# A tuned transformer block on one core: tile 1 in two pieces, x2 and x3 loaded behind weight block 2, tiles 4 to 7 normalized in pairs, the Gelu table preloaded, four DMA transposes ahead of the stores

## Chip, cores, metric

One core of one Trainium2 chip. The metric is the device time of one execution in us. A ratio is the mean time of one kernel's runs over that of the other's of the same rounds, so it is not quite the ratio of the medians quoted. The profile covers a somewhat shorter span than the device time (227.4 against 229.1 us for one run of the kernel before).

## The reference

```python
xn = layernorm(x)                       # x: 2048 x 512, bf16
s  = window_attention(xn, wqkv) @ wo    # 32 heads of 16, 8 keys at distances 0, 2, .. 14
g  = silu((gelu(xn @ w_gate) * (xn @ w_up)) @ w_down)   # 512 -> 1792 -> 512
return x + s * g
```

## The kernel before

The 2048 rows are worked on in four row blocks of four tiles of 128 rows. Each row block is normalized, transposed (xnT), projected to q, k, v, and goes through the gated layer and the attention. Row block 0's first projection is done half a row block at a time, so that it can begin when tiles 0 and 1 are there. x0 to x3 are the tiles as loaded. "Weight block k" (w0 to w3) is wqkv's rows 128k to 128k+127; one pass over it is 12 matmuls of 256 columns ("block k" below). It is multiplied with chunk k of each tile, that is the tile's columns 128k to 128k+127 after the transpose.

```python
    for i in range(2):                       # loads: x0 x1 w0 w1 x2 x3 w2 w3
        for t in (2 * i, 2 * i + 1):
            load_x(t)
        for k in (2 * i, 2 * i + 1):
            nc.sync.dma_start(out=wqkv_sb[:, k, :], in_=A_wqkv[k * P : (k + 1) * P, :])
    # ... cut: the other loads, constants ...
    first_stats(0); first_moments(0); first_stats(1); first_rstd(0); first_moments(1)
    normalize(0)
    transpose(0)                             # TensorE into PSUM, ScalarE copies to xnT
    first_rstd(1)
    normalize(1)
    warm_up(4, P)                            # matmuls on constants
    transpose(1, parts=2, copy=nc.vector.tensor_copy)
    for t in (2, 3):
        first_stats(t); first_moments(t)     # sqrt on ScalarE
    for t in (2, 3):
        first_rstd(t); normalize(t)
    for dk in range(NC):                     # blocks 0..3 for tiles 0 and 1
        for n, (fo, ps) in enumerate(pairs): # 2 pairs of v, 4 of q and k
            # ... cut: two matmuls on xnT[0][:, dk, 0:256] ...
            if dk == 2 and n in (2, 5):
                transpose(2 + (n == 5), copy=nc.vector.tensor_copy)
    for fo, ps in pairs:
        copy_out(0, fo, ps, 0, HQ, 2, nc.vector.tensor_copy if fo >= 8 else None)
    for t in range(TPQ, 2 * TPQ):
        moments(t)                           # then normalize(4..7) in the next loop
    # ... cut: second half (tiles 2 and 3), 48 matmuls into qkv_ps ...
    # block 1 and on: per-stage side work
    at(("glu", 1, 0), transpose_by_dma, 2 * TPQ + i)   # i = 0..3, SyncE's queue
    at(("glu", 2, 0), transpose_by_dma, 3 * TPQ + i)
```

The softmax here doesn't subtract the row's maximum and nothing guards it: scores larger than these inputs give would overflow.

## Time and profile before

| | kernel before | changed kernel |
|---|---|---|
| median, lowest to highest (us) | 229.41, 228.83 to 229.80 (6 runs) | 228.49, 228.35 to 229.03 (6 runs) |
| span of the profile | 227.4 | 226.7 |
| first useful matmul starts | 6.55 | 6.27 |
| second half of the projection starts | 12.45 | 11.98 |
| second u group of the gated layer starts | 20.93 | 20.25 |

(A u group is the four matmuls with w_up for 128 of the 1792 columns; a g group those with w_gate.) Three lines from the timeline of TensorE, kernel before (start, length, engine, line, operation, operands, count, in brackets the idle time and what ended it):

```profile
6.55 0.60 PE L554 MATMUL v_ps<-xnT,wqkv_sb 128*128 128x256 bf16 x4 [0.48 <-DVE xnT L225]
9.37 0.61 PE L554 MATMUL v_ps<-xnT,wqkv_sb 128*128 128x256 bf16 x4
12.45 0.27 PE L249 MATMUL qkv_ps<-xnT,wqkv_sb 128*128 128x256 bf16 x1
```

They are the starts of block 0, of block 2 and of the second half. A block without a wait takes 1.31 us, four transposes 0.22 us.

### The profile page before, as it was taken

What the parts mean: (1) busy time and instruction counts of PE and PEld (TensorE: products, weight loads), DVE (VectorE), ACT (ScalarE), POOL (GpSimd) and SP (SyncE); (2) the same over time, 40 slices, a digit from 0 to 9 for tenths busy, and PEclk for the clock granted to TensorE, in tenths of its full rate; (3) what the DMA queues carried; (4) which work ended last, traced back from release to release, by engine and by line L of the source; (5) the groups of instructions that cost most, each with busy time, mean ns of one, the idle gap of its engine ahead of it and who ended that gap; (6) DMA issues with size and microseconds to landing.
All of it is one profiled execution on the core that took longest, in us unless ns stands there. A gap on an engine that the chain in (4) does not pass through costs nothing.

```text
span 227.4 us, 3595 instructions
## 1 busy us (share of the span) xinstructions
PE 222.3 (98%) x1326; PEld 107.1 (47%) x1326; DVE 151.8 (67%) x278; ACT 132.2 (58%) x209; POOL 25.0 (11%) x67
## 2 busy tenths in 40 slices
PE   8999999999999999999999999999999999999993
PEld 4785444444444444444444444444444444444453
DVE  4696981899995588969904759924934348971434
ACT  4279769777531676766751466767763356756210
POOL 1027901000040000333700000000000000000000
PEclk9999999999999999999999999999999999999998
DMA  6999499941039911100219921100217950000011
GB/s 206 349 395 384 127 201 142 321 109 67 28 83 202 223 25 25 29 10 0 92 33 206 214 71 29 26 18 0 81 26 151 197 140 0 0 0 22 12 37 56
DMA packets 30130, 24.64 MB, mean 108 GB/s; under 512 B 10784, under 2 KB 29600, under 8 KB 30112
## 3 DMA queue, kind: packets, MB, share of 16 engines
q1 hardware_dynamic: 30112, 24.41, 44.3%
q8 instruction: 10, 0.16, 0.3%
q14 instruction: 8, 0.07, 0.1%
HBM read 18.74 MB, written 4.34 MB: 102 GB/s over the span
## 4 chain that ended last, share of the span: by engine, by line
PE 95%; DVE 1%; ACT 1%; DMA 1%; issue 0%; DVEq 0%
PE y_ps L443 21%; PE u_ps L249 21%; PE g_ps L249 21%; PE qkv_ps L249 16%; PE s_ps L459 6%; PE L_ps L338 3%; PE o_ps L406 3%; PE qk_ps L554 2%; DMA x_sb<-in_A_x_dram 1%; PE v_ps L554 1%; ACT L431 1%; DVE stats L182 1%; PE tr L214 1%; PE den_ps L358 0%; ACT ge L431 0%; ACT vst L273 0%
## 5 line engine op out<-in xcount | busy, mean ns | idle before, releaser
L249 PE MATMUL u_ps<-xnT,wu_sb 128*128 128x512 bf16 x224 | 57.5, 379 | 0.0
L249 PE MATMUL g_ps<-xnT,wg_sb 128*128 128x512 bf16 x224 | 57.5, 379 | 0.0
L443 PE MATMUL y_ps<-wd_sb,h 128*128 128x512 bf16 (+1 forms) x238 | 49.9, 367 | 0.0
L435 DVE TENSOR_TENSOR h<-ge,u 128x512 bf16<-128x512 bf16 x56 | 23.8, 425 | 30.7 <-ACT u L433 29.0
L433 ACT ACTIVATE u<-u_ps 128x512 bf16<-128x512 f32 x56 | 33.5, 598 | 16.4 <-PE u_ps L249 16.4
L431 ACT ACTIVATE ge<-g_ps 128x512 bf16<-128x512 f32 x56 | 33.5, 598 | 16.2 <-PE g_ps L249 16.0
L320 DVE TENSOR_TENSOR pk<-q_sb,k_sb 128x1024 bf16<-128x1024 bf16 (+1 forms) x56 | 38.9, 762 | 4.6 <-ACT k_sb L273 4.6
L392 DVE TENSOR_TENSOR pv<-E,v_arr 128x1024 bf16<-128x1024 bf16 (+1 forms) x48 | 39.8, 863 | 0.2 <-issue 0.2
L249 PE MATMUL qkv_ps<-xnT,wqkv_sb 128*128 128x512 bf16 (+1 forms) x192 | 37.0, 352 | 0.0
L443 PEld LDWEIGHTS <-h 128*128 128x128 bf16 x238 | 23.0, 98 | 25.9 <-issue 1.3
L249 PEld LDWEIGHTS <-wu_sb 128*128 128x128 bf16 x224 | 21.9, 98 | 26.6 <-issue 0.3
L249 PEld LDWEIGHTS <-wg_sb 128*128 128x128 bf16 x224 | 21.7, 98 | 26.3 <-issue 0.8
L451 ACT ACTIVATE sl<-y_ps 128x512 bf16<-128x512 f32 (+1 forms) x17 | 9.7, 572 | 32.6 <-PE y_ps L443 32.6
L249 PEld LDWEIGHTS <-wqkv_sb 128*128 128x128 bf16 x192 | 18.8, 98 | 17.5
L467 DVE TENSOR_TENSOR m<-s_ps,sl 128x512 bf16<-128x512 f32 (+1 forms) x17 | 11.1, 655 | 17.0 <-PE s_ps L459 17.0
L418 DVE TENSOR_TENSOR oT<-o_ps,rb 128x1024 bf16<-128x1024 f32 x8 | 9.4, 1220 | 13.8 <-DMA rb<-rs_d 13.8
L199 POOL TENSOR_TENSOR rstd<-rstd,mhalf 128x1 f32<-128x1 f32 x12 | 8.0, 663 | 69.9 <-DVE rstd L196 69.9
L459 PE MATMUL s_ps<-wo_sb,oT 128*128 128x512 bf16 (+1 forms) x68 | 14.8, 366 | 0.0
L273 ACT ACTIVATE vst<-qkv_ps 128x512 bf16<-128x512 f32 x14 | 8.4, 597 | 3.7 <-PE qkv_ps L249 3.7
L273 ACT ACTIVATE k_sb<-qkv_ps 128x512 bf16<-128x512 f32 x14 | 8.4, 601 | 3.2 <-PE qkv_ps L249 3.2
L273 ACT ACTIVATE q_sb<-qkv_ps 128x512 bf16<-128x512 f32 x14 | 8.3, 603 | 3.0 <-PE qkv_ps L249 3.0
L459 PEld LDWEIGHTS <-oT 128*128 128x128 bf16 x68 | 6.7, 98 | 7.2
(57 smaller groups left out, 131.4 us busy)
## 6 DMA issues: line engine op xcount, KB each, us to landing
v_arr<-vT SPq DMA_DIRECT2D x16, 520.0 KB, 8.5
vT<-vst SPq DMA_DIRECT2D x8, 256.0 KB, 2.2
out_dram<-o_t SPq DMA_DIRECT2D x15, 128.0 KB, 3.4
wg_sb<-in_B_w_gate_dram SPq DMA_DIRECT2D x2, 896.0 KB, 10.1
wu_sb<-in_B_w_up_dram SPq DMA_DIRECT2D x2, 896.0 KB, 11.0
wd_sb<-in_B_w_down_dram SPq DMA_DIRECT2D x1, 1792.0 KB, 11.5
wqkv_sb<-in_A_wqkv_dram SPq DMA_DIRECT2D x4, 384.0 KB, 4.9
x_sb<-in_A_x_dram SPq DMA_DIRECT2D x3, 512.0 KB, 10.5
```

Source lines behind the costliest of these rows:

```text
L249: nc.tensor.matmul(ps, lhsT=w[:, dk, lo : lo + P], rhs=xnT[j][:, dk, i0 : i0 + n], start=(dk == 0), stop=(dk == NC - 1),)
L273: nc.scalar.activation(out=dst, in_=ps, func=AF.Copy)
L320: nc.vector.tensor_tensor(out=st[j]["pk"][w][:, c0 : c0 + n, :], in0=st[j]["q"][:, c0 : c0 + n, :], in1=k_sb[j][:, c0 : c0 + n, off : off ...
L392: nc.vector.tensor_tensor(out=pv[:, d : d + n, :], in0=st[j]["E"][:, wh, :].unsqueeze(1).to_broadcast([P, n, TQ]), in1=st[j]["va"][:, 4 * ...
L418: nc.vector.tensor_tensor(out=oT[:, g : g + 2, :], in0=st[j]["o"][:, g : g + 2, :], in1=st[j]["rb"][:].unsqueeze(1).to_broadcast([P, 2, TQ ...
L431: nc.scalar.activation(out=ge[:], in_=g_ps[:], func=AF.Gelu_apprx_tanh)
L433: nc.scalar.activation(out=u[:], in_=u_ps[:], func=AF.Copy)
L435: nc.vector.tensor_tensor(out=h[:], in0=ge[:], in1=u[:], op=ALU.mult)
L443: nc.tensor.matmul(y[:], lhsT=st[j][fc][:, tt * P : (tt + 1) * P], rhs=wd_sb[:, fc, cols], start=(fc == 0), stop=(fc == NF - 1),)
L451: nc.scalar.activation(out=sl[:], in_=y[:], func=AF.Silu)
L459: nc.tensor.matmul(s[:], lhsT=st[j]["oT"][:, g, tt * P : (tt + 1) * P], rhs=wo_sb[:, g, cols], start=(g == 0), stop=(g == NC - 1),)
L467: nc.vector.tensor_tensor(out=m[:], in0=s[:], in1=sl[:], op=ALU.mult)
```

## The change

The intent is to begin sooner (VectorE handles chunk 0 of tile 1 first, since block 0 reads only chunk 0 of the transposed x), not to wait for w2, to take the table load out of ScalarE's busy time, and to give SyncE's long row of transposes a start ahead of the output stores. Tile 0's copy is split likewise, two of the warm-up matmuls (on constants, to keep TensorE busy) go, and tiles 4 to 7 are normalized two at a time. The core of the diff:

```diff
+    for t in (0, 1):
+        load_x(t)
+    for k in range(NC - 1):
+        load_wqkv(k)
+    for t in (2, 3):
+        load_x(t)
+    load_wqkv(NC - 1)
 ...
-    transpose(0)
+    to_psum(0)
+    from_psum(0, [0])
+    from_psum(0, rest)
+    warm_up(2, P)
     first_rstd(1)
-    normalize(1)
-    warm_up(4, P)
-    transpose(1, parts=2, copy=nc.vector.tensor_copy)
+    normalize(1, [0])
+    normalize(1, rest)
+    to_psum(1, [0])
+    from_psum(1, [0], nc.vector.tensor_copy)
+    to_psum(1, rest)
+    from_psum(1, rest, nc.vector.tensor_copy)
 ...
+    nc.scalar.preload_act_table(AF.Gelu_apprx_tanh)
 ...
-            if dk == 2 and n in (2, 5):
-                transpose(2 + (n == 5), copy=nc.vector.tensor_copy)
+            if (dk, n) in ((2, 5), (3, 2)):
+                transpose(dk, copy=nc.vector.tensor_copy)
 ...
-    for t in range(TPQ, 2 * TPQ):
-        moments(t)
+    for t in range(TPQ, 2 * TPQ, 2):
+        for fn in (moments, normalize):
+            fn(t)
+            fn(t + 1)
 ...
-        at(("glu", 1, 0), transpose_by_dma, 2 * TPQ + i)
+        at(("glu", 1, 0) if i else ("down", 0, 3), transpose_by_dma, 2 * TPQ + i)
-        at(("glu", 2, 0), transpose_by_dma, 3 * TPQ + i)
+        at(("glu", 2, 0) if i else ("down", 1, 3), transpose_by_dma, 3 * TPQ + i)
```

More of the change, by code (lines that the diff above doesn't have):

```diff
@@ L96, in load_w, with load_wqkv @@
         )
-    for i in range(2):
-        for t in (2 * i, 2 * i + 1):
-            load_x(t)
-        for k in (2 * i, 2 * i + 1):
-            nc.sync.dma_start(out=wqkv_sb[:, k, :], in_=A_wqkv[k * P : (k + 1) * P, :])
+    def load_wqkv(k):
+        nc.sync.dma_start(out=wqkv_sb[:, k, :], in_=A_wqkv[k * P : (k + 1) * P, :])
+    for t in (0, 1):
[5 more added lines that the diff above has]
+    load_wqkv(NC - 1)
     load_x(TPQ, TPQ)
@@ L201, with normalize, to_psum, from_psum @@
     xns = {}
-    def normalize(t):
-        xn = xns[t] = xnp.tile([P, D], BF16, name="xn")
+    def normalize(t, cs=range(NC)):
+        if 0 in cs:
+            xns[t] = xnp.tile([P, D], BF16, name="xn")
+        cols = slice(cs[0] * P, (cs[-1] + 1) * P)
         nc.vector.tensor_scalar(
-            out=xn[:], in0=x_sb[:, t, :], scalar1=mv[:, t, 0:1], scalar2=rstd[:, t, :],
+            out=xns[t][:, cols], in0=x_sb[:, t, cols],
+            scalar1=mv[:, t, 0:1], scalar2=rstd[:, t, :],
             op0=ALU.subtract, op1=ALU.mult,
         )
-    def transpose(t, parts=1, copy=None):
-        xn = xns[t]
-        tr = mm.tile([P, NC * P], BF16, name="tr", tag="mm")
-        for c in range(NC):
-            nc.tensor.transpose(tr[:, c * P : (c + 1) * P], xn[:, c * P : (c + 1) * P], ident[:])
+    trs = {}
+    def to_psum(t, cs=range(NC)):
+        if 0 in cs:
+            trs[t] = mm.tile([P, NC * P], BF16, name="tr", tag="mm")
+        for c in cs:
+            nc.tensor.transpose(
+                trs[t][:, c * P : (c + 1) * P], xns[t][:, c * P : (c + 1) * P], ident[:]
+            )
+    def from_psum(t, cs=range(NC), copy=None):
         j, i = divmod(t, TPQ)
-        if i == 0:
+        if j not in xnT:
             xnT[j] = xtp.tile([P, NC, TQ], BF16, name="xnT")
-        dst = xnT[j][:, :, i * P : (i + 1) * P]
-        src = tr[:].rearrange("p (c n) -> p c n", c=NC)
-        for k in range(parts):
-            c = slice(k * NC // parts, (k + 1) * NC // parts)
-            if copy is None or k % 2:
-                nc.scalar.activation(out=dst[:, c], in_=src[:, c], func=AF.Copy)
-            else:
-                copy(out=dst[:, c], in_=src[:, c])
+        c = slice(cs[0], cs[-1] + 1)
+        dst = xnT[j][:, c, i * P : (i + 1) * P]
+        src = trs[t][:].rearrange("p (c n) -> p c n", c=NC)[:, c]
+        if copy is None:
+            nc.scalar.activation(out=dst, in_=src, func=AF.Copy)
+        else:
+            copy(out=dst, in_=src)
+    def transpose(t, copy=None):
+        to_psum(t)
+        from_psum(t, copy=copy)
     def warm_up(n, cols):
@@ L482 @@
     for i in range(TPQ):
-        at(("qkv", 0, i), normalize, TPQ + i)
         at(("down", 0, 1), moments, 2 * TPQ + i)
@@ L533 @@
     warm_up(4, P)
+    rest = range(1, NC)
     first_stats(0)
@@ L560 @@
                 )
-            if dk == 2 and n in (2, 5):
-                transpose(2 + (n == 5), copy=nc.vector.tensor_copy)
+            if (dk, n) in ((2, 5), (3, 2)):
+                transpose(dk, copy=nc.vector.tensor_copy)
     for fo, ps in pairs:
         copy_out(0, fo, ps, 0, HQ, 2, nc.vector.tensor_copy if fo >= 8 else None)
-    for t in range(TPQ, 2 * TPQ):
-        moments(t)
+    for t in range(TPQ, 2 * TPQ, 2):
+        for fn in (moments, normalize):
+            fn(t)
+            fn(t + 1)
     sum_constants()
     for n, fo in enumerate((0, 2, 4, 6, 8, 10)):
-        if n < TPQ:
-            run("qkv", 0, n)
         ps = mm.tile([P, 2, HQ], F32, name="qkv_ps", tag="mm")
```

## The prediction

> **What bounds the kernel now.** I read the page's busy shares first, then the chain that ended last in order of time, then the timelines of TensorE and VectorE over the first 21 us, and at last the queue of SyncE.
>
> ```profile
> PE 222.3 (98%) x1326; PEld 107.1 (47%) x1326; DVE 151.8 (67%) x278; ACT 132.2 (58%) x209; POOL 25.0 (11%) x67
> PE 95%; DVE 1%; ACT 1%; DMA 1%; issue 0%; DVEq 0%
> ```
>
> TensorE is busy 222.3 of the 227.4 us of the span, and it is 95% of the chain. Idle time is therefore at most 5.1 us, and the table by stretches puts 1.55 us of it in the first 12 us and 3.51 us after 220 us (the last multiply, add and store, which the change leaves alone). A change that takes no matmul away can win only what TensorE loses at its head. The chain says where that is:
>
> ```profile
> 5.69 0.40 PE tr L214 x4
> 6.09 0.02 issue
> 6.12 0.30 DVE xnT L225
> 6.42 0.14 issue
> 6.55 0.60 PE v_ps L554 x4
> ...
> 17.89 0.60 ACT vst L273
> 18.48 0.49 ACT xnT L223
> 18.97 0.02 issue
> 18.99 1.28 ACT L431
> 20.27 0.01 issue
> 20.28 0.61 ACT ge L431
> 20.89 0.04 issue
> 20.93 1.02 PE u_ps L249 x4
> ```
>
> Columns are start, length, what. The first useful matmul starts at 6.55, when VectorE has copied tile 1 out of PSUM. From there TensorE runs without a break, but for two places. One is at 20.93: four 512-column matmuls start every 0.86 us in the whole middle of the kernel, the group before started at 19.86, so this one was due at 20.72 and is 0.21 us late. It waits for a PSUM buffer, since ScalarE spends 1.28 us loading the Gelu table first. The other is in the first pass over weight blocks 0 to 3:
>
> ```profile
> 9.36 0.55 PEld L554 LDWEIGHTS <-wqkv_sb 128*128 128x128 bf16 x6 [0.31 <-DMA wqkv_sb<-in_A_wqkv_dram]
> 8.19 0.69 DVE L182 BATCH_NORM_STATS2 stats<-x_sb 128x6 f32<-128x512 bf16 x1 [0.62 <-DMA x_sb<-in_A_x_dram]
> 9.19 0.41 DVE L205 TENSOR_SCALAR xn<-x_sb,mv,rstd 128x512 bf16<-128x512 bf16 x1
> 9.71 0.41 DVE L205 TENSOR_SCALAR xn<-x_sb,mv,rstd 128x512 bf16<-128x512 bf16 x1
> ```
>
> These are from the two timelines; the bracket is idle time and what ended it. Blocks 0 and 1 start at 6.55 and 7.86, so a block is 12 matmuls in 1.31 us; block 2 was due at 9.17 and starts at 9.37, having waited for its weights: 0.20 us. Tile 3 of x landed just before 8.19, and tiles 2 and 3 are normalized 1.41 and 1.93 us after that. The completion records in the trace give the landings in full: x0 2.92, x1 3.25, w0 5.29, w1 6.32, x2 6.64, x3 8.17, w2 9.32, w3 10.32 us.
>
> Block 1 of the work needs its DMA transposes by about 98.5 us:
>
> ```profile
> 73.05 3.52 SPq L470 DMA_DIRECT2D out_dram<-o_t  x4
> 76.62 20.72 SPq L241 DMA_TRANSPOSE xnT<-xn  x16
> ```
>
> In SyncE's queue 16 transposes follow the four stores, 1.30 us each, and the last is issued at 96.1 and lands some 2.3 us later, at 98.4. The matmuls that read them start at 98.53 and the last chunk is read three matmuls (0.65 us) later. No wait shows, but the margin is under 1 us.
>
> **What the Trainium skill says.** "ScalarE: Activation LUTs", section "What ACT_TABLE_LOAD costs", has about 1283 ns for a table load and some 1380 ns of drain. The trace agrees on the load (1.28 us here) and shows no such drain: the load starts 0.02 us after the copy before it. "DMA: Bandwidth & Descriptors", section "Queues, rings and completion order", says each DMA engine consumes descriptors in ring order, and that a transfer is complete only when all its engines are. The trace agrees: of w2's 16 completions 14 are in by 7.9 us and two come at 9.2 and 9.3, so the slowest engine sets the landing. "Perfetto Trace Analysis", section "Optimizing Scalar/DVE Operations", says that breaking up instructions can let work complete sooner where those engines are not saturated but cause bubbles. That is what the two pieces of tile 1 do; the trace of before already splits tile 1's copy in two halves, and the first half is what TensorE waits for.
>
> **The change, part by part.**
>
> Tile 1 in two pieces. VectorE normalizes 512 columns in 0.41 us and a one-column operation of that kind takes 0.15, so 128 columns are about 0.21 us (straight line between the two, an estimate). Start stays 5.21: piece one ends at 5.42, the other three chunks at about 5.75. TensorE transposes chunk 0 from 5.49 and its result is out 0.22 us later (the mean of one 128-column transpose), at 5.71. Copies out of PSUM took 0.29 us for 256 columns and 0.42 for 512, so 0.23 for 128: it starts behind the second normalize, 5.77 to 6.00. With the 0.13 us that lay between copy and matmul before, the first matmul starts at about 6.1 instead of 6.55: **0.4 us earlier**. The remaining chunks are copied by about 6.5, and block 1, which needs them, comes at 6.1 + 1.31 = 7.4, so they are hidden. Two warm-up matmuls fewer take nothing from this: matmuls are at 221 ns, full speed, since 4.46, and no gap is longer than about 0.3 us.
>
> x2 and x3 behind block 2. The order is now x0 x1 w0 w1 w2 x2 x3 w3. w2 comes earlier; x3 now ends at the place in the stream where w2 ended, the same 1.70 MB, so it should land at w2's old 9.3 us if the two slow engines are slow again, and near 8.0 if not. w3 stays at 10.3. Block 2 would start at 6.1 + 2.62 = 8.7, and its weights should be there: the 0.20 us wait goes. But tile 2's transpose stands at the end of block 2, at 8.7 + 1.31 = 10.0. It needs x3 + 1.41 us (VectorE does the statistics of both tiles first), plus 0.05:
> - x3 at 9.3: transpose at 10.8, block 3 at 11.0 (four transposes are 0.22 us), tile 3's transpose after six matmuls at 11.7, its copy done at 11.7 + 0.39 + 0.04 + 0.42 = 12.55, the second half of the projection at 12.67. It started at 12.45 before. Loss 0.2.
> - x3 at 9.0: everything 0.3 earlier, 12.35. Gain 0.1.
> - x3 at 8.3 or less: block 3 waits for w3 until 10.3, the second half starts at about 12.0. Gain 0.45.
> So what the first two parts save is largely spent waiting for x3. I choose 12.25, a gain of **0.2 us**.
>
> Gelu table preloaded. The load now stands behind the square roots of tiles 2 and 3, at about 10.5, and ends near 11.8; ScalarE was idle 3.21 us before 12.64. The load at 18.99 goes, the first Gelu can follow the copy at 18.97, and the wait at 20.93 goes with it: **0.21 us**, not 1.28, as the rest of the load was beside matmuls.
>
> Normalizing tiles 4 to 7 in pairs on VectorE waits for GpSimd's power (0.55 us each) perhaps twice, some 0.7 us, and starts about 0.6 later. The first product of q and k moves from 18.18 to about 20. VectorE had 2.0 us idle before 21.40, so this fills a hole. The last product ended at 32.9 before and the matmuls that read it start at 33.97; back to back it ends near 33. Nothing on the path.
>
> Four DMA transposes ahead of the stores, twice. At 1.3 us each they fit between the end of the v loads (68.0) and the first store (73.05). They carry the end of the 16 from 98.4 to about 93. TensorE was not waiting in this trace, so **0 us** here; in runs where the transposes are slower it may remove a short wait. I allow 0.1.
>
> Sum: 0.2 + 0.2 + 0.1 = 0.5 us off 229.31, so **228.8 us**, 0.2%.
>
> **Rivals.** First, x3 becomes the bound: late again through a slow engine, the pass ends 0.2 us later than before, and the table's 0.2 us only cancels it: 229.3. For it: w2 landed late at this very place, and two engines of 16 made it so. Second, x3 is on time and all parts add up: 0.45 + 0.2 + 0.1, 228.5. For it: 14 of 16 engines were through at 7.9. Third, the moved transposes delay v loads or stores, or the later VectorE work makes the logits late. Against it: the transposes stand behind the v loads in the same ring order, four output tiles are buffered, and 1 us of margin lies before the logits; it would make 229.5 to 230. Against any of them being large: all of TensorE's idle time before 220 us is 1.6 us, of which 0.8 is before the first instruction.
>
> **Range and chances.** The three runs of before spread from 228.83 to 229.8, so a median of few runs can be off by some 0.3 us, and the rivals span 228.5 to 229.5. Eight in ten: 228.1 to 229.5. Two per cent is 4.6 us, more than the head of the kernel has to give or, failing a new long wait, to lose: within 2% at 0.98, faster 0.01, slower 0.01.
>
> **What would show it.** Right: the first matmul on v at about 6.1; no table load between 18 and 21 us, matmul groups there every 0.86 us plus the transposes; block 2 without a wait for weights; a wait of TensorE for the normalized tile 2 near 10 us; second half of the projection near 12.25. Wrong: x2 and x3 landing before 8 us with block 3 then waiting for w3, a first matmul not earlier than 6.4, a new wait at the logits near 34 us, or any wait in the middle that the old chain didn't have.

## The result, and the profile after

228.49 us against 229.41 us; the ratio is 0.9967, with a 95% interval of 0.9949 to 0.9986. That is within 2% and a third of a per cent faster, inside the predicted range.

The busy line of TensorE on the page after, then the chain that ended last in order of time, changed kernel (start, length, what):

```profile
PE 221.7 (98%) x1324; PEld 107.0 (47%) x1324; DVE 152.4 (67%) x280; ACT 132.1 (58%) x209; POOL 20.1 (9%) x67
```

```profile
5.82 0.23 DVE xnT L238
6.06 0.04 issue
6.10 0.33 PE tr L224 x3
6.43 0.44 PE v_ps L578 x4
...
12.12 5.26 PE qkv_ps L266 x48
...
19.55 0.86 PE g_ps L266 x4
20.41 0.86 PE u_ps L266 x4
```

(Once TensorE runs without a break the chain counts by ends, so its starts lie 0.1 to 0.2 us behind those of the timeline.) The copies and the table load of ScalarE that stood between 17.89 and 20.93 are gone from the chain. From 6.10 to 223.22 it is TensorE alone. At its head is something new: the chunk-0 copy on VectorE is followed by three transposes, and only then by the first useful matmul. From the timelines of TensorE and VectorE, changed kernel:

```profile
8.71 0.69 DVE L187 BATCH_NORM_STATS2 stats<-x_sb 128x6 f32<-128x512 bf16 x1
9.70 0.41 DVE L212 TENSOR_SCALAR xn<-x_sb,mv,rstd 128x512 bf16<-128x512 bf16 x1
10.20 0.39 PE L224 MATMUL tr<-ident,xn 128*128 128x128 bf16 x4
11.98 5.40 PE L266 MATMUL qkv_ps<-xnT,wqkv_sb 128*128 128x256 bf16 x48
```

Tile 2 is normalized at 10.11 and its transpose starts at 10.20, when it is due (block 2 started at 8.89, and 8.89 + 1.31 = 10.20). It did not wait, with 0.1 us to spare. The completion records of this trace give w2 7.45, x2 7.76, x3 8.68, w3 9.67 us.

So the 0.69 us between the two spans is: 0.28 at the first matmul, 0.19 more up to the second half (the wait for w2 of 0.20 is gone), and 0.21 at the second u group (6.55 - 6.27, then 12.45 - 11.98 less 0.28, then 20.93 - 20.25 less 0.47). From there on the two timelines stay 0.68 to 0.69 us apart to the end.

The queue of SyncE, changed kernel, row block 1:

```profile
67.35 5.28 SPq L258 DMA_TRANSPOSE xnT<-xn  x4
72.73 6.36 SPq L487 DMA_DIRECT2D out_dram<-o_t  x4
79.15 15.39 SPq L258 DMA_TRANSPOSE xnT<-xn  x12
```

The row ends at 94.54, against 76.62 + 20.72 = 97.34 before: 2.8 us earlier, 0.7 of it because the whole kernel runs that much earlier (in row block 2 the row ends 4.2 us earlier). The transposes fit ahead of the stores, but the four stores then take 6.36 us instead of 3.52. They do not wait for their data: VectorE has finished the last output tile at 75.51, and its store is issued at 78.76. What holds the queue no view shows.

### The profile page after: what moved, and what is told of

It is laid out like the page before. It is cut to its first block, busy times and chain, and to the rows that moved or that the text cites. A ratio compares the mean times of both kernels' runs of the same rounds, so it can differ in the third digit from the quotient of the medians.

```text
span 226.7 us, 3599 instructions
## 1 busy us (share of the span) xinstructions
PE 221.7 (98%) x1324; PEld 107.0 (47%) x1324; DVE 152.4 (67%) x280; ACT 132.1 (58%) x209; POOL 20.1 (9%) x67
## 4 chain that ended last, share of the span: by engine, by line
PE 96%; DVE 1%; DMA 1%; issue 0%; ACT 0%; DVEq 0%
PE y_ps L460 21%; PE g_ps L266 21%; PE u_ps L266 21%; PE qkv_ps L266 16%; PE s_ps L476 6%; PE L_ps L355 3%; PE o_ps L423 3%; PE qk_ps L578 2%; DMA x_sb<-in_A_x_dram 1%; PE v_ps L578 1%; PE tr L224 1%; DVE stats L187 1%; PE den_ps L375 0%; DVE m L484 0%; DVE mv L190 0%
```

## Experiments

The theory after this reading: the head is a chain of waits of which only the last counts, the order of loads takes a late w2 out of it, and the moved transposes add margin, not time. The rivals: the parts gain independently; the order of loads gives nothing of itself; the transposes were waited for in some runs.

### The parts alone

Each is the kernel before plus one part of the change; all four ran on one chip beside 11 runs of the kernel before (228.79 to 230.08).

**Tile 1 in two pieces** (with two warm-up matmuls fewer).

```diff
-    transpose(0)
+    to_psum(0); from_psum(0, [0]); from_psum(0, rest); warm_up(2, P)
     first_rstd(1)
-    normalize(1); warm_up(4, P); transpose(1, parts=2, copy=nc.vector.tensor_copy)
+    normalize(1, [0]); normalize(1, rest)
+    to_psum(1, [0]); from_psum(1, [0], nc.vector.tensor_copy)
+    to_psum(1, rest); from_psum(1, rest, nc.vector.tensor_copy)
```

> The kernel before with tile 1 in two pieces alone (and two warm-up matmuls fewer). Theory (the waits follow each other, the last one counts): the first v matmul starts at 6.27 us as in the changed kernel, 0.28 earlier than before, but block 2's weights still land near 9.3, so block 2 starts no earlier than before (9.37) and the second half of the projection stays within 0.1 of 12.45; span 227.2 to 227.5, time ratio 0.999 to 1.001. Should w2 land earlier in this run, block 2 follows the landing. Rival (the parts add up, each its own): second half at 12.17, span 0.28 shorter, 227.1.

Measured: 228.97 us, ratio 0.9997 (0.9982 to 1.0012). First matmul at 6.22; w2 landed at 8.89 in the profiled run and block 2 started at 8.93, due at 8.84, so the second half came at 12.01. This one trace has the gain, since w2 happened to be early; over the six runs there is none that can be told from zero.

**The order of loads** (with the later places of the transposes of tiles 2 and 3).

```diff
+    # the loads as in the change: x0 x1 w0 w1 w2 x2 x3 w3
-            if dk == 2 and n in (2, 5):
-                transpose(2 + (n == 5), copy=nc.vector.tensor_copy)
+            if (dk, n) in ((2, 5), (3, 2)):
+                transpose(dk, copy=nc.vector.tensor_copy)
```

> The kernel before with the order of loads and the later transposes alone. Theory: first v matmul at 6.55 as before, w2 lands near 7.4 so that block 2 starts at 9.17 without a wait (0.20 gained), x3 lands near 8.7 and tile 2 is normalized by 10.1, before its transpose is due at 10.48; second half at 12.27 (12.45 before), span 227.2, ratio 0.998 to 1.000. Rival: the later x3 is waited for and eats the gain, second half at 12.45 or later and a wait of TensorE for the normalized tile.

Measured: 229.54 us, ratio 1.0016 (1.0001 to 1.0030): alone this part is slower, if anything. w2 landed at 7.37, x3 at 8.25, and block 2 did not wait, as the theory has it. Two things went otherwise. The clock of TensorE rose late in this run (the trace's clock record has the full clock from 5.71 us on, against 4.29 in the kernel before), so the transposes at 5.06 took 0.63 us for four instead of 0.40, and the first matmul came at 6.90, 0.35 late; the second half came at 12.61, 0.34 later than the expected 12.27. And a new wait appeared, from TensorE's timeline:

```profile
18.15 0.40 PE L219 MATMUL tr<-ident,xn 128*128 128x128 bf16 x4
```

The transpose of tile 4 was due at 12.61 + 5.23 = 17.84 and starts 0.31 us later, when VectorE has normalized tile 4. VectorE copies v only after tile 3's chunk, which is now later, and then does the statistics of four tiles before it normalizes the first. The pairing of tiles 4 to 7 in the change takes this wait away, as a run below shows; the prediction had counted it as off the path.

**The Gelu table.**

```diff
         first_moments(t)
+    nc.scalar.preload_act_table(AF.Gelu_apprx_tanh)
```

> The kernel before with the preload of the Gelu table alone. Theory: the load of 1.28 us moves to about 9.5 us, where ScalarE has nothing to do, and the third u matmul group starts at 20.72 instead of 20.93; the start at 12.45 is unchanged; span 0.21 shorter, 227.15; ratio 0.998 to 1.000. Rival 1: the whole 1.28 us is saved. Rival 2: the load delays the copies of the projection or a second load comes later, nothing saved.

Measured: 229.04 us, ratio 0.9994 (0.9979 to 1.0009). w2 landed at 9.82 in the profiled run, so the second half came at 12.95, not 12.45, and the span is longer than before. The step itself is clear in the chain:

```profile
20.52 0.86 PE g_ps L249 x4
21.39 0.65 PE u_ps L249 x3
```

On TensorE's timeline the u group follows the g group after 0.86 us (20.36 to 21.22), where it was 1.07 before (19.86 to 20.93): the 0.21 us is gained and no more. (It is the second u group; the expectation calls it the third.)

**The DMA transposes.**

```diff
-        at(("glu", 1, 0), transpose_by_dma, 2 * TPQ + i)
+        at(("glu", 1, 0) if i else ("down", 0, 3), transpose_by_dma, 2 * TPQ + i)
```

> The kernel before with the four DMA transposes ahead of the stores alone, in both blocks. Theory: TensorE waits for no transpose in the kernel before, so nothing changes: same starts at 12.45, 98.53 and 152.39, span 227.3 to 227.4, ratio 0.999 to 1.001; the last transpose of the 16 is issued about 2 to 5 us earlier than the old 96.1. Rival: some of the runs before that took 229.5 to 229.8 had waited for late transposes, and this kernel has none of these: ratio below 0.998 and a smaller spread, with nothing changed in the trace.

Measured: 229.28 us, ratio 1.0005 (0.9990 to 1.0020), 228.81 to 229.52. Its profiled run had w2 at 8.45 and the second half at 12.24; the starts in the later row blocks are shifted by that same 0.21 us (98.16 against 98.37, for one). So this part gains nothing on its own, and nothing here shows that late transposes make the spread of the runs before. The four parts alone add up to a ratio of 1.0012; together, with the pairing, they have 0.9967, so they do not gain independently, as far as intervals of some 0.0015 to either side of each ratio tell.

### Parts taken out of the change

**Without the pairing.**

```diff
-    for t in range(TPQ, 2 * TPQ, 2):
-        for fn in (moments, normalize):
-            fn(t); fn(t + 1)
+    for t in range(TPQ, 2 * TPQ):
+        moments(t)               # normalize(4..7) after all four
```

> The changed kernel with the statistics of tiles 4 to 7 all ahead of their normalizing, as before, everything else of the change kept. Theory from the run of the load order alone, where the first transpose of tile 4 came 0.31 us late: with v's two copies now behind tile 3's, VectorE normalizes tile 4 near 17.5 us (15.46 in the changed kernel) and TensorE, due for its transpose 5.23 us after the start of the second half (17.2), waits about 0.3 us; span 226.9 to 227.1, some 0.3 above the changed kernel at the same landings and clock. Rival (the prediction's view that the pairing is off the path): no wait there, span as the changed kernel's, 226.7.

Measured: 228.81 us, ratio 0.9991 (0.9977 to 1.0005). VectorE and TensorE, timelines:

```profile
17.52 1.37 DVE L212 TENSOR_SCALAR xn<-x_sb,mv,rstd 128x512 bf16<-128x512 bf16 x4
17.98 0.40 PE L224 MATMUL tr<-ident,xn 128*128 128x128 bf16 x4
```

The second half began at 12.43 (again a late clock), so the transpose was due at 17.66: 0.32 us of waiting, as expected. The wait is real and the pairing removes it.

**The old order of loads in the changed kernel.**

```diff
-    for k in range(NC - 1):
+    for k in range(2):
         load_wqkv(k)
     for t in (2, 3):
         load_x(t)
-    load_wqkv(NC - 1)
+    for k in range(2, NC):
+        load_wqkv(k)
```

> The changed kernel with the loads in the old order (x2 and x3 ahead of weight blocks 2 and 3), everything else kept. Theory: w2 lands anywhere from 8.4 to 9.9 us, as in the four runs with that order, block 2 is due at about 8.9 and starts at the landing if that is later; the second half starts at the later of 11.98 and the landing + 2.66 to 2.7; span 226.7 to 227.6, a wider spread than the changed kernel's, ratio to before 0.997 to 1.000. Rival: the order of loads gives nothing of itself and the time is the changed kernel's.

Measured: 229.17 us, ratio 1.0002 (0.9982 to 1.0021), the six runs from 228.58 to 229.95. From TensorE's timeline, its block 2:

```profile
9.98 0.61 PE L579 MATMUL v_ps<-xnT,wqkv_sb 128*128 128x256 bf16 x4 [0.44 <-DMA wqkv_sb<-in_A_wqkv_dram]
```

w2 landed at 9.93 in this run. The second half came at 13.08, 3.1 us behind block 2 and not the 2.66 to 2.7 that I had written down; I had left out the transposes of tiles 2 and 3, twice 0.22 us. Without the changed order all other parts together gain nothing that these runs show, and the spread (1.37 us) is wider than the changed kernel's (0.68 in its first six runs, 0.18 in its second six).

The landings over all traces say why. With the old order w2 landed at 8.21, 8.45, 8.89, 9.32, 9.82 and 9.93 us; with the new order at 7.37 to 7.94 (eight traces, the one with x2 and x3 last among them), for a block due at 8.8 to 9.5. x3, which now ends where w2 ended in the stream, landed at 8.25 to 8.68 in the other seven of these. It is not the place of w2 alone: w3, last of the eight in both orders, landed at 9.21 to 10.92 us with the old order and at 9.24 to 9.72 with the new. Why the stream is so unsteady with the old order stays open. In the kernel before two of w2's 16 completions (one from each DMA engine) came 1.3 and 1.4 us behind the other 14, and two of w3's 1.2 and 1.3 us behind its other 14, but what held up those two engines no run here shows.

**x2 and x3 behind all weights.**

```diff
-    for k in range(NC - 1):
+    for k in range(NC):
         load_wqkv(k)
     for t in (2, 3):
         load_x(t)
-    load_wqkv(NC - 1)
```

> The changed kernel with x2 and x3 behind all four weight blocks. Theory: x3 lands near 9.7, tile 2 is normalized 1.43 us later at 11.1 and its transpose, due at 10.20, waits until then: 1.0 us, so that second half starts near 12.9 instead of 11.98 and the span is 227.6. That is the first rival of the prediction, made to happen. Against it: if x3 lands near 9.0 the wait is 0.3 us, and if nothing depends on x3 the start stays at 11.98.

Measured: 229.78 us, ratio 1.0033 (1.0017 to 1.0050). From TensorE's timeline:

```profile
11.49 0.40 PE L223 MATMUL tr<-ident,xn 128*128 128x128 bf16 x4 [0.75 <-DVE xn L211]
```

Due at 9.27 + 1.31 = 10.58, the transpose of tile 2 starts at 11.49: 0.91 us of waiting for the normalized tile. x2 and x3 landed at 9.21 and 9.56, only 0.35 us apart, so VectorE had not finished tile 2's statistics when x3 came, and the time from x3 to the normalized tile was 1.88 us (end at 11.44), not 1.43. This is the first rival of the prediction, made to happen: x can be loaded too late, and 0.9 us later than in the changed kernel's first trace is too late.

### The new wait at the head

The new order of reading and writing in one PSUM tile is visible in the chain after: chunks 1 to 3 of tile 1 were normalized by 5.79 us, but TensorE transposes them at 6.10 only, when VectorE has copied chunk 0 out of the same tile. The Trainium skill, "PSUM — Partial Sum Buffer", section "PSUM bank collisions raise a hardware error", says that TensorE may not write a bank of PSUM (the memory that TensorE writes its results to) while VectorE reads the same quadrant of 32 partitions of it, whatever the columns, and that software has to keep the two apart, by bank and quadrant or simply by bank. That fits the wait: it lies between accesses that share no byte. It would also fit a program that orders accesses by tile; the test below does not tell these apart, since its new tile is also a new bank. The test gives chunk 0 a bank of its own, and takes the second bank of v later in exchange.

```diff
+    trs[1] = mm.tile([P, NC * P], BF16, name="tr", tag="mm")   # between chunk 0 and the rest
     to_psum(1, rest)
     from_psum(1, rest, nc.vector.tensor_copy)
+    pairs.insert(1, (10, mm.tile([P, 2, HQ], F32, name="v_ps", tag="mm")[:]))
 ...
-                    start=False,
+                    start=(fo == 10 and dk == 0 and i == 0),
```

In the first attempt I also normalized tile 2 ahead of tile 3's statistics.

> The changed kernel with tile 1's first chunk in a PSUM bank of its own, the second v bank taken later in exchange, and tile 2 normalized before tile 3's statistics. Theory: the wait of 0.32 us ahead of the transposes of chunks 1 to 3 is there because they write the bank that VectorE reads; with another bank they run at about 5.8, the first v matmul starts at 6.15 instead of 6.27, and all that follows 0.12 earlier if no load is waited for: second half at 11.86, span 226.56. Rival: the first matmul is bound by something else (the weights' landing or the copy of tile 0 at 6.07) and stays at 6.27.

Measured: 228.98 us, ratio 0.9997 (0.9982 to 1.0011). TensorE's timeline:

```profile
5.51 0.71 PE L224 MATMUL tr<-ident,xn 128*128 128x128 bf16 x4
6.24 0.60 PE L582 MATMUL v_ps<-xnT,wqkv_sb 128*128 128x256 bf16 x4
...
11.62 0.40 PE L224 MATMUL tr<-ident,xn 128*128 128x128 bf16 x4 [0.42 <-DVE xn L212]
```

The wait between chunks is gone: four transposes run in one row and the first matmul follows at 6.24, though the clock rose only at 6.05. But my own addition lost it again. With one tile after the other VectorE waits twice for ScalarE's square root (0.36 us each), tile 3 is ready at 11.56, and its transpose, due 0.87 us after that of tile 2 at 10.16, is 0.59 us late (the expectation of the run with the bank alone, below, puts it at 0.48). Two tiles' statistics side by side were better.

> The changed kernel once more, for comparison on the chip and in the rounds of the three others. Theory: its start is set by the copy of tile 1's chunk and by when the clock of TensorE rises; with a rise before 5 us the second half of the projection starts at 11.98, with a rise near 6 us at 12.4 to 12.5, as in the run without the pairing; span 226.7 to 227.2, ratio to before 0.995 to 0.999.

> The changed kernel with tile 1's first chunk in a PSUM bank of its own alone, the statistics of tiles 2 and 3 left as in the change (their new order cost 0.48 us of waiting ahead of tile 3's transpose in the run before). Theory: no wait ahead of chunks 1 to 3, first v matmul at 6.15 with an early clock and 6.25 with a late one (6.27 and 6.65 to 6.75 in the changed kernel), tile 2 normalized at x3 + 1.43; second half at 11.9 to 12.0, or where x3 lands at 8.7 or later 1.43 + 1.9 behind it; span 226.5 to 226.7; ratio to the changed kernel 0.998 to 1.000. Rival: the tenth of a us gained is waited for at tile 2's transpose, no gain in the end.

The changed kernel again: 228.79 us, ratio to before 0.9977 (0.9964 to 0.9990), the six runs from 228.70 to 228.88. Its clock rose at 6.71 us, the first matmul came at 6.76 and the second half at 12.48. Only the bank changed: 228.58 us, ratio to before 0.9969 (0.9953 to 0.9985). Its TensorE timeline:

```profile
6.19 0.60 PE L580 MATMUL v_ps<-xnT,wqkv_sb 128*128 128x256 bf16 x4
11.90 5.40 PE L266 MATMUL qkv_ps<-xnT,wqkv_sb 128*128 128x256 bf16 x48
```

It has the shortest span of all the traces (226.6) with a clock that rose at 5.12, and no wait ahead of tile 2 or 3. The mean of its six runs is 228.62, that of the changed kernel in the same rounds 228.79, less than the spread of the runs: that the wait is gone is shown, that the kernel is faster for it is not.

### How much margin the transposes had

Two transposes of no use were put into SyncE's queue, in the kernel before and in the changed kernel alike. They copy two chunks of a normalized tile into constants that are no longer read, and the results of both kernels stayed correct.

```diff
+        if i == 1:                  # ahead of tile 9's transposes, and of tile 13's
+            at(("glu", 1, 0), extra_transposes, 2 * TPQ + i)
+            at(("glu", 2, 0), extra_transposes, 3 * TPQ + i)
```

> The kernel before with two more DMA transposes, of no use, in SyncE's queue ahead of tile 9's and of tile 13's. Theory: the last transposes land at 98.4 and 152.5 and are read at 99.2 and 153.0, so the margins are 0.8 and 0.5 us; 2 x 1.3 us more makes TensorE wait 1.8 and 2.1 us, span 231.3, ratio 1.015 to 1.018. Rival: the transposes have more slack than the trace tells, or the two extra ones overlap with others, and the ratio is under 1.005.

> The changed kernel with the same two extra transposes. Theory: the four transposes ahead of the stores made the margins about 2.9 and 4.1 us, so that 2.6 us more just fit: waits under 0.4 us in all, ratio to before 0.996 to 1.000, against 1.015 or more for the same load on the kernel before. Rival: moving the four only moved the stores, and the wait is as long as there.

The kernel before with them: 234.29 us, ratio 1.0217 (1.0182 to 1.0252), slower beyond doubt, though at the mark of 2% the verdict is unclear. The changed kernel with them: 228.73 us, ratio 0.9967 (0.9947 to 0.9987), as without. TensorE at the start of row block 2's projection, first the kernel before, then the changed one:

```profile
98.30 0.59 PE L255 MATMUL qkv_ps<-xnT,wqkv_sb 128*128 128x512 bf16 x2
99.84 0.38 PE L255 MATMUL qkv_ps<-xnT,wqkv_sb 128*128 128x512 bf16 x1 [0.94 <-DMA xnT<-xn]
101.08 2.10 PE L255 MATMUL qkv_ps<-xnT,wqkv_sb 128*128 128x512 bf16 x9 [0.86 <-DMA xnT<-xn]
```

```profile
98.19 5.13 PE L272 MATMUL qkv_ps<-xnT,wqkv_sb 128*128 128x512 bf16 x23
```

In the kernel before the third and fourth matmul each wait for a chunk of the last tile. They would have been due 0.22 us after one another, so the fourth, due at 98.95, is 2.1 us late; in row block 3 the same happens, 2.2 us (157.13 instead of 154.94). That was 1.8 and 2.1 in the expectation. So the kernel before stood within about half a us of a wait at two places that no view shows as one, and the change removes this. The four timed runs lost 5.0 us on the mean (0.0217 of 229.3), and the profiled one, the fastest of them, about 4 us: the 4.3 us of the two waits account for that one, but not for the rest of the others.

## Why the prediction was right

It was right in the range, and in where TensorE loses time; its number came near in part by luck. It forecast 0.2 + 0.2 + 0.1 = 0.5 us, and the traces have 0.47 + 0.21 + 0 = 0.68. In the first term two errors have opposite sign: the first matmul came 0.17 us later than forecast, and the wait for x3 that was to eat most of the gain did not come. In the last term 0.1 us was allowed and nothing came. So what happened is the prediction's second rival, x3 on time and the parts adding up, with 228.5; and of its signs of being right two did not appear, the wait for tile 2 near 10 us and a second half near 12.25. The prediction's bound from idle time was also read too low: a group's tail counts as busy, so the 0.21 us wait at 20.93 stands there as 0.04.

- **Tile 1 in two pieces**: predicted 0.4 us (first matmul at about 6.1), measured 0.28 (6.27). The copy of chunk 0 ended at 6.05 where 6.00 was predicted. What failed is the step "The remaining chunks are copied by about 6.5 ... so they are hidden". Their copies were hidden (they ended at 6.83, ahead of block 1 at 7.58), but not their transposes: the program issues these ahead of the first matmul, and they had to wait for the copy, so 0.17 us of transposes came between the copy and the first matmul. With the bank changed the first matmul came at 6.19. That two warm-up matmuls fewer "take nothing from this" is not shown; see the clock below.
- **x2 and x3 behind block 2**: the wait for w2 went, as predicted. "What the first two parts save is largely spent waiting for x3" did not happen: x3 landed at 8.68, not at 9.0 to 9.3, tile 2 was ready 1.43 us later as predicted (10.11), and the transpose due at 10.20 did not wait. The step that failed was to give x3 w2's late landing because it has w2's place in the stream; seven traces have it at 8.25 to 8.68. The second half started at 11.98, predicted 12.25. It is also not the prediction's third case ("x3 at 8.3 or less"), which has this start by a wait for w3: w3 landed at 9.67, before block 3 was due at 10.42. That x3 is the next bound was right: it had 0.1 us to spare, and its later load made TensorE wait. (That a transfer is complete only when all its engines are stands one section further on that page than the prediction says, with the 16 increments of a DMA's semaphore.)
- **Gelu table**: predicted 0.21 us, measured 0.21, in the change and alone.
- **Tiles 4 to 7 in pairs**: "Nothing on the path" was right for the changed kernel (first product of q and k at 19.41, predicted about 20, no wait at the logits). Missed was that the change needs it: without it TensorE waits 0.32 us.
- **DMA transposes**: no gain, as predicted, and the allowance of 0.1 us for slow runs found no support. The end of the row was predicted at 5.4 us earlier and came 2.8 us earlier, because the stores behind the four took longer. The margin that the prediction read from the trace, "under 1 us", was right to a few tenths.
- **What the prediction took as fixed** is the start of the kernel before. It allowed for a late or early x3 and for the spread of the times, but the profiled landing of w2, 9.32, is one of six between 8.21 and 9.93, and the profiled rise of the clock, 4.29, one of many. The measured gains of 0.76 us (0.0033 of 229.4) and 0.53 us (0.0023, in the later rounds) lie around the 0.69 us of the two traces. Two parts, the two pieces and the preload, were never taken out of the change, so their shares rest on the starts in the traces.

The clock is another part of the unsteadiness. By the traces' clock records it rose at 3.90 to 6.71 us in the 14 traces. In the seven with the two pieces in one bank the first matmul came at 6.22 and 6.27 where the clock rose at 4.50 and 3.90, and at 6.65 to 6.77 where it rose at 5.79 to 6.71; in the changed kernel that moved the second half from 11.98 to 12.48. Nine traces of kernels with two warm-up matmuls at that place have 3.90 to 6.71, five with four have 3.90 to 5.71. Whether the two matmuls less delay the clock is left open. The records hint at another reason: the full clock lasts 221.87 us in 13 traces and 225.28 in the longest, 3.41 us more, and 221.87 is 65 times 3.413. The clock seems to change in steps of 3.41 us that do not begin with the kernel, and the spread of 2.8 us lies within one step. This is inferred from these figures and not tested. The single sizes above, which come from one trace each, are compared at their own due times for this reason.

## What to carry to other kernels

Where one engine is busy 98% of the time, look for gains only where it starts, and follow the starts of three or four of its groups through the head: a gain counts only if the next load is there too, so a part that is worth 0.3 us alone can be worth nothing until another part removes the wait behind it. Read a landing from more than one trace before a due time is set against it; a reordered load may be worth more by its steadiness than by its mean. And test a margin by using it up: two transposes of no use, put into each kernel, told in one pair of runs what no wait in the profile could show.

## What the Trainium skill lacked or had wrong

- "TensorE: Matmul & The Clock Gate", section "What you observe", has the transition around 4 us into sustained matmul activity, give or take 500 ns; here, with the first matmul at 0.84 us, the full clock came 3.1 to 5.9 us after it in 14 traces (3.90 to 6.71 us of the span), a spread of 2.8 us. The page's next section, "What's actually happening", is nearer: it has a window of 3413 ns that does not start with the kernel, and the two lengths of the full clock above agree with that.
- "ScalarE: Activation LUTs", section "What ACT_TABLE_LOAD costs", adds a drain of some 1380 ns to every switch to another set of tables; in the kernel before the load at 18.99 started 0.02 us after the copy before it and the first Gelu 0.01 us after the load: 1.28 us in all.
- No page says how unsteady one load is: 393 KB of weights at one place in one stream landed between 8.21 and 9.93 us in six traces. It would belong to "DMA: Bandwidth & Descriptors".
